# An attention and two-layer-pair kernel: PSUM sums in banks chosen by block, y1 split straight from PSUM, and attention, q and the later layers at other steps of a block

## The chip, the cores and the metric

One core of one Trainium2 chip. The time is device microseconds (us) of one execution, lower is better. Six engines matter: TensorE (PE, with its weight loads PEld), VectorE (DVE), ScalarE (ACT), GpSimd (POOL), and SyncE (SP), whose queue issues the DMAs.

## The reference, cut to what matters

```python
kv_pool = kv.reshape(B, H//r, r, W//r, r, C).mean(axis=(2, 4))   # 768 keys
k = v = kv_pool.reshape(B, -1, C) @ w_sr
a = softmax((q @ k.T) / sqrt(C));  x = a @ v                      # 12288 tokens, C = 128
h = x @ w_in1;  g = max(h, 0) + alpha * min(h, 0);  x = g @ w_out1   # 128 -> 2048 -> 128
h = x @ w_in2;  g = h * sigmoid(1.702 * h);         out = g @ w_out2  # 128 -> 2048 -> 128
```

## The kernel before

The 12288 tokens are worked in 24 blocks of 512. Every product is made of three fp16 matmuls (`mm3`: high by high, high by low, low by high), so each operand is split into a scaled high part (ACT) and a low part (DVE or POOL). A block j has five stages: attention (S, the scores, four sets of 128 tokens; V, the six groups of keys summed into `xacc`), L1 and L2 of the first pair (`h1`, then the sum `y1`), L3 and L4 of the second pair (`h3`, then the sum `y2`). L1 to L4 run over 16 slices m of the 2048 inner columns.

The program is written as steps t, 16 to a block. In step t stands slice m of L1 for t = 16j + m; L2 comes 4 steps later, L3 `L3_LAG` steps later, L4 `L4_LAG` steps later, so that five blocks' stages are mixed: in the middle of the run each step has three matmuls of each of L1, L4, L3 and L2, in this order on PE, 12 of 512 columns, with S or V matmuls between L4 and L3. "Step s" below is s = t mod 16. `ATT_START` is the step at which a block's attention begins, `ATT_S` and `ATT_V` are the places of its S sets and V groups behind that. For each S set DVE takes the maximum (`nm`), ACT the exponential (`s`) with its sum, DVE the reciprocal (`r`), ACT the scaled high part (`ah`), DVE the low part (`al`); both go through transposing DMAs into V's operands.

Before q, `xacc` and `y1` are split, their largest value is taken (`ta` on DVE), spread over the partitions by a one-column matmul (`qt`, `pt`, `yt`), and turned into a power of two. `x_scale` and `x_split`, `a_q` and `q_split`, `y_scale` and `y_split` do this; `parts` makes the two halves (ACT, then DVE).

The eight PSUM banks before: two for S, one (`ps_x`) shared in turn by `xacc`, `qt` and `yt`, two (`ps_y`) shared in turn by `y1` and `y2`, three (`ps_h`) shared in turn by `h1`, `h3` and `pt`. A bank of such a ring is given to the third-next allocation, in the order of the code, once DVE's instruction that reads it last is done (L347 for `h1`, L402 for `h3`). When L2 of a block ends, ACT copies `y1` to SBUF (`yc`, L372) and the split works on the copy.

The framework's scheduler fixes at build time the order of the instructions on each engine; each engine then works strictly in that order and waits for semaphores. POOL makes the low part of `g1` and, for three of four slices, of `g2` (`g1l`, `g2l`); the rest of `g2l` is DVE's.

Of the kernel before, what the change touches and what calls it, by code (L numbers as in the profile page):

```python
# [10 lines left out]
F32 = mybir.dt.float32  # L11
# [23 lines left out]

L2_LAG, L3_LAG, L4_LAG = 4, 31, 36

ATT_START = [-18, -5] + [KF * j - 25 for j in range(2, NB)]  # L40
ATT_S = [(0, 2, 2, 6), (0, 3, 6, 9)] + [(0, 4, 7, 12)] * (NB - 2)
ATT_V = [(5, 8, 9, 12), tuple(range(12, 18))] + [(17, 18, 19, 21, 22, 22)] * (NB - 2)
KV_FREE = -11
W4_LOAD = -8

# [8 lines left out]
def attn_moe_kernel(ctx: ExitStack, tc: tile.TileContext, q, kv, w_sr, w_in1, w_out1, alpha, w_in2, w_out2, out):  # L54
    nc = tc.nc
# [5 lines left out]
    at_p = ctx.enter_context(tc.tile_pool(name="atp", bufs=2))  # L61
    e_p = ctx.enter_context(tc.tile_pool(name="ep", bufs=2))
    t_p = ctx.enter_context(tc.tile_pool(name="tp", bufs=2))
    ps_s = ctx.enter_context(tc.tile_pool(name="ps_s", bufs=1, space=PSUM))
    ps_x = ctx.enter_context(tc.tile_pool(name="ps_x", bufs=1, space=PSUM))
    ps_y = ctx.enter_context(tc.tile_pool(name="ps_y", bufs=2, space=PSUM))

    first = ExitStack()
    ps_w = first.enter_context(tc.tile_pool(name="ps_w", bufs=1, space=PSUM))
    ps_s2 = first.enter_context(tc.tile_pool(name="ps_s2", bufs=1, space=PSUM))  # L70
    ps_h = None

# [19 lines left out]
    kyc = const.tile([P, 1], F32, name="kyc")  # L92
# [9 lines left out]
    def mm3(o, wh, wl, xh, xl, start, stop):  # L102
        mm(out=o, lhsT=wh, rhs=xh, start=start, stop=False)  # L103
        mm(out=o, lhsT=wh, rhs=xl, start=False, stop=False)  # L104
        mm(out=o, lhsT=wl, rhs=xh, start=False, stop=stop)  # L105

    def ts(out, in0, s1, op0, s2=None, op1=None):
        if op1 is None:
            nc.vector.tensor_scalar(out=out, in0=in0, scalar1=s1, scalar2=None, op0=op0)
        else:  # L110
            nc.vector.tensor_scalar(out=out, in0=in0, scalar1=s1, scalar2=s2, op0=op0, op1=op1)

    def small(name, dt=F32, w=1):
        return sm_p.tile([P, w], dt, tag=name, name=name)
# [88 lines left out]
    late = []  # L203
# [5 lines left out]
    qh, ql, qsc, xacc, eh, el, xh, xl, xsc = ({} for _ in range(9))  # L209
# [6 lines left out]
    def q_split(j):  # L216
        src = q_t.pop(j)
        qh[j] = at_p.tile([P, TB], F16, tag="qh", name="qh")
        ql[j] = at_p.tile([P, TB], F16, tag="ql", name="ql")
        c, p = scale_of(qsc[j], ps_x.tile([P, TB], F32, tag="x", name="qt"), None, "q")  # L220
        qsc[j] = p
        late.append(lambda: parts(qh[j], ql[j], src, c))

# [60 lines left out]

    def a_v(j, k):
        if k == 0:
            xacc[j] = ps_x.tile([P, TB], F32, tag="x", name="xacc")
        if j == 0:

            ts_ = slice(k * P, (k + 1) * P)  # L290
            for i in range(KT):
                mm3(xacc[j][:, ts_], v_hi[:, i, :], v_lo[:, i, :], eh[j][:, i, ts_], el[j][:, i, ts_],
                    i == 0, i == KT - 1)
        else:
            mm3(xacc[j], v_hi[:, k, :], v_lo[:, k, :], eh[j][:, k, :], el[j][:, k, :], k == 0, k == KT - 1)
        if k == len(ATT_V[j]) - 1:
            d = small("xd", BF16)
            xsc[j] = d
            late.append(lambda: top_of(xacc[j], d))

    def top_of(x, d):

        a = small("ta")
        nc.vector.tensor_reduce(out=a, in_=x, axis=AX.X, op=ALU.max, apply_absolute_value=True)
        ts(d, a, 2.0 ** -60, ALU.max)

    def scale_of(d, pm, kc, name):

        mm(out=pm[:, 0:1], lhsT=ones, rhs=d, start=True, stop=True)
        p, c = (sm_p.tile([P, 1], I32, tag=name + x, name=name + x, bufs=4) for x in "pc")  # L310

        def f():
            ts(p, pm[:, 0:1].bitcast(I32), 0x7F800000, ALU.bitwise_and)
            ts(c, p, -1.0, ALU.mult, float(268 << 23) if kc is None else kc, ALU.add)

        late.append(f)
        return c.bitcast(F32), p.bitcast(F32)

    def parts(hi, lo, x, c):
        nc.scalar.activation(hi, x, AF.Copy, scale=c)  # L320
        nc.vector.scalar_tensor_tensor(out=lo, in0=x, scalar=c, in1=hi, op0=ALU.mult, op1=ALU.subtract)
# [212 lines left out]
    def at(t, lag):  # L534

        j, m = divmod(t - lag, KF)
        return (j, m) if 0 <= j < NB else None

    def step(t):
        pieces = [(j, t - ATT_START[j]) for j in range(NB) if -8 < t - ATT_START[j] < 26]  # L540
        if x := at(t, L2_LAG):
            l2(*x)
        flush()
        if x := at(t, 2):
            l1_split(*x)
        if x := at(t, L3_LAG + 1):
            l3_act(*x)
        if x := at(t, L3_LAG + 2):
            l3_split(*x)
        if x := at(t, 0):  # L550
            l1(*x)
        if x := at(t, L4_LAG):
            l4(*x)
        flush()
        for j, p in pieces:
            for n, p0 in enumerate(ATT_S[j]):
                if p == p0 + 1:
                    a_e(j, n)
                elif p == p0 + 2:
                    a_h(j, n)  # L560
                elif p == p0 + 3:
                    a_l(j, n)
        flush()
        for j, p in pieces:
            for n, p0 in enumerate(ATT_S[j]):
                if p == p0:
                    a_s(j, n)
            for k, p0 in enumerate(ATT_V[j]):
                if p == p0:
# [75 lines left out]
```

## Time and profile before

| what | before |
|---|---|
| time, median of 3 runs | 1294.55 us (1293.88 to 1294.94) |
| the profiled execution | 1294.28 us, its span from first to last instruction 1292.5 us |
| PE busy | 1228.2 us (95%) |
| ACT busy | 1107.2 us (86%) |
| DVE busy | 1036.0 us (80%) |
| POOL busy | 780.6 us (60%) |
| matmuls | 5784 |
| granted TensorE clock, mean | 0.979 |

Busy is the time in which an engine had an instruction in work, without its waits. Matmuls overlap in the records (a 512-column one is shown with 0.38 us and the next begins 0.21 to 0.22 us later), so PE's idle time is seen better from the starts of neighbours than from the busy share. The kernel has a start (loads, the keys, the weights of the first pair), a ramp in which the blocks fill the steps, 20 or so equal blocks, and a tail in which only the second pair is left.

### The profile page before, as it was taken

To read this page: it belongs to the slowest core of one execution; us is meant where nothing else is said; L and a number is where in the kernel's file an instruction comes from. 1 tells how busy PE (TensorE), PEld (TensorE's weight loads), DVE (VectorE), ACT (ScalarE), POOL (GpSimd) and SP (SyncE) were. 2 spreads that over 40 slices of the span, in tenths; PEclk is the share of its full clock that TensorE was granted. 3 is DMA by queue.
4 is the path that set the end of the run, shared out by engine and by line. 5 is a ranking of instruction groups with operands and counts; after the bars stand their busy time and mean duration, and the time that the engine had idled before them with its cause. 6 is when DMAs were issued, how large, how long until landed. Compare 5 with 4: busy or idle time off the path is not lost.

```text
span 1292.5 us, 18032 instructions
## 1 busy us (share of the span) xinstructions
PE 1228.2 (95%) x5784; PEld 567.1 (44%) x5784; DVE 1036.0 (80%) x1879; ACT 1107.2 (86%) x1964; POOL 780.6 (60%) x670
## 2 busy tenths in 40 slices
PE   3468999999999999999999999999999999999998
PEld 2323444444444444444444444444444444444443
DVE  7988899778788787887887787787888878877666
ACT  1477899899898898898898998998988988988998
POOL 1046535576675676666665665756756666667774
PEclk8678999999999999999999999999999999999999
DMA  9713312122121221211221121221212212110000
GB/s 374 169 43 56 62 33 54 37 41 54 25 54 42 37 54 33 45 42 37 48 48 38 42 54 30 49 47 32 53 33 46 49 32 43 34 37 21 9 9 17
DMA packets 165375, 66.65 MB, mean 52 GB/s; under 512 B 156448, under 2 KB 156576, under 8 KB 164256
## 3 DMA queue, kind: packets, MB, share of 16 engines
q1 hardware_dynamic: 165280, 65.51, 21.9%
q8 instruction: 45, 0.74, 0.2%
q14 instruction: 50, 0.41, 0.1%
HBM read 21.05 MB, written 6.29 MB: 21 GB/s over the span
## 4 chain that ended last, share of the span: by engine, by line
PE 55%; ACT 16%; DVE 13%; issue 5%; DMA 0%; POOLq 0%; ACTq 0%
PE h L103 8%; PE h L105 7%; PE h L104 7%; PE y L104 7%; PE y L105 7%; PE y L103 7%; DVE g L347 4%; ACT g L346 4%; ACT g L401 3%; ACT s L255 3%; DVE g L402 2%; ACT g1h L354 2%; PE xacc L103 2%; PE xacc L104 2%; PE xacc L105 2%
## 5 line engine op out<-in xcount | busy, mean ns | idle before, releaser
L355 POOL TENSOR_TENSOR g1l<-g,g1h 128x512 f16<-128x512 f32 x384 | 457.0, 1196 | 324.9 <-ACT g1h L354 308.8
L411 POOL TENSOR_TENSOR g2l<-g,g2h 128x512 f16<-128x512 f32 x272 | 315.4, 1160 | 120.5 <-ACT g2h L409 110.9
L401 ACT ACTIVATE g<-h,yu 128x512 f32<-128x512 f32 x384 | 269.4, 702 | 103.9 <-PE h L105 100.8
L402 DVE SCALAR_TENSOR_TENSOR g<-g,h 128x512 f32<-128x512 f32 x384 | 262.5, 684 | 110.6 <-ACT g L401 104.9
L347 DVE SCALAR_TENSOR_TENSOR g<-g,oma,h 128x512 f32<-128x512 f32 x384 | 284.9, 742 | 53.1 <-ACT g L346 47.1
L354 ACT CAST g1h<-g 128x512 f16<-128x512 f32 x384 | 244.3, 637 | 7.2 <-PE y L105 5.6
L346 ACT ACTIVATE g<-h 128x512 f32<-128x512 f32 x384 | 236.2, 615 | 15.3 <-PE h L105 8.0
L409 ACT CAST g2h<-g 128x512 f16<-128x512 f32 x384 | 243.8, 635 | 3.3 <-PE y L105 1.2
L104 PE MATMUL y<-g1l,w2h 128*128 128x512 f16 x384 | 145.5, 379 | 8.7 <-POOL g1l L355 8.7
L103 PE MATMUL h<-xh,w1h 128*128 128x512 f16 x384 | 146.5, 383 | 5.2 <-ACT xh L320 4.1
L103 PE MATMUL h<-yh,w3h 128*128 128x512 f16 x384 | 145.2, 378 | 4.2 <-DVE g L347 1.1
L104 PE MATMUL h<-xl,w1h 128*128 128x512 f16 x384 | 146.6, 382 | 1.4
L105 PE MATMUL h<-xh,w1l 128*128 128x512 f16 x384 | 146.7, 382 | 0.0
L103 PE MATMUL y<-g1h,w2h 128*128 128x512 f16 x384 | 145.6, 379 | 1.2 <-ACT g1h L354 1.2
L104 PE MATMUL y<-g2l,w4h 128*128 128x512 f16 x384 | 145.5, 379 | 0.5 <-POOL g2l L411 0.5
L105 PE MATMUL y<-g2h,w4l 128*128 128x512 f16 x384 | 145.5, 379 | 0.0
L105 PE MATMUL y<-g1h,w2l 128*128 128x512 f16 x384 | 145.5, 379 | 0.0
L103 PE MATMUL y<-g2h,w4h 128*128 128x512 f16 x384 | 145.5, 379 | 0.0
L105 PE MATMUL h<-yh,w3l 128*128 128x512 f16 x384 | 145.4, 379 | 0.0
L104 PE MATMUL h<-yl,w3h 128*128 128x512 f16 x384 | 145.3, 378 | 0.0
L245 DVE TENSOR_REDUCE nm<-s 128x1 f32<-128x768 f32 x96 | 91.5, 953 | 14.2 <-PE s L240 10.6
L411 DVE TENSOR_TENSOR g2l<-g,g2h 128x512 f16<-128x512 f32 x112 | 90.0, 804 | 9.7 <-ACT g2h L409 9.7
(227 smaller groups left out, 1664.8 us busy)
## 6 DMA issues: line engine op xcount, KB each, us to landing
q<-in_q SPq DMA_DIRECT2D x24, 256.0 KB, 2.6
kv<-in_kv SPq DMA_DIRECT2D x12, 512.0 KB, 9.9
out<-ob SPq DMA_DIRECT2D x24, 256.0 KB, 2.0
raw_w<-in_moe_w_in SPq DMA_DIRECT2D x4, 1024.0 KB, 9.7
raw_w<-in_moe_w_out SPq DMA_DIRECT2D x4, 1024.0 KB, 6.9
eh<-ah SPq DMA_TRANSPOSE x96, 2.7
wsr<-in_w_sr SPq DMA_DIRECT2D x1, 64.0 KB, 2.7
al<-in_moe_alpha SPq DMA_DIRECT2D x1, 8.0 KB, 1.8
```

The source lines that it names most:

```text
L103: mm(out=o, lhsT=wh, rhs=xh, start=start, stop=False)
L104: mm(out=o, lhsT=wh, rhs=xl, start=False, stop=False)
L105: mm(out=o, lhsT=wl, rhs=xh, start=False, stop=stop)
L245: nc.vector.tensor_reduce(out=nm, in_=s[:, :, 0:HALF], axis=AX.XY, op=ALU.max, negate=True)
L346: nc.scalar.activation(g, h, AF.Relu, scale=-1.0)
L347: nc.vector.scalar_tensor_tensor(out=g, in0=g, scalar=oma[:, m:m + 1], in1=h, op0=ALU.mult, op1=ALU.add)
L354: nc.scalar.copy(hi, g)
L355: nc.gpsimd.tensor_tensor(out=lo, in0=g, in1=hi, op=ALU.subtract)
L401: nc.scalar.activation(g, h, AF.Tanh, scale=ysc[j][:, 0:1])
L402: nc.vector.scalar_tensor_tensor(out=g, in0=g, scalar=1.0, in1=h, op0=ALU.add, op1=ALU.mult)
L409: nc.scalar.copy(hi, g)
L411: e.tensor_tensor(out=lo, in0=g, in1=hi, op=ALU.subtract)
```

## The change

Three things are done.

1. Banks. `ps_x` and `ps_y` become one pool of three banks: `xacc` and `y1` of block j are summed in bank j mod 2 (first the one, then the other), `y2` of every block in the third. `qt` and `yt` go to the ring of three that `h1`, `h3` and `pt` use (before the first step, to the single bank of the start).
2. `y1` is no longer copied to SBUF: `ta` and the split read it from PSUM, the split one step earlier.
3. Steps. L3 and L4 run 28 and 33 steps behind L1, not 31 and 36; the last S set 10 and not 12 steps behind the attention's begin, V one step earlier; q is prepared 8 steps earlier, `x` scaled and split one step earlier.

```diff
-L2_LAG, L3_LAG, L4_LAG = 4, 31, 36
+L2_LAG, L3_LAG, L4_LAG = 4, 28, 33
-ATT_S = [(0, 2, 2, 6), (0, 3, 6, 9)] + [(0, 4, 7, 12)] * (NB - 2)
-ATT_V = [(5, 8, 9, 12), tuple(range(12, 18))] + [(17, 18, 19, 21, 22, 22)] * (NB - 2)
+ATT_S = [(0, 2, 2, 6), (0, 3, 6, 9)] + [(0, 4, 7, 10)] * (NB - 2)
+ATT_Q = [None, (-6, -4), (-6, -4)] + [(-14, -12)] * (NB - 3)
+ATT_V = [(5, 8, 9, 12), tuple(range(12, 18))] + [(16, 17, 18, 19, 20, 21)] * (NB - 2)
...
-    ps_x = ctx.enter_context(tc.tile_pool(name="ps_x", bufs=1, space=PSUM))
-    ps_y = ctx.enter_context(tc.tile_pool(name="ps_y", bufs=2, space=PSUM))
+    ps_a = ctx.enter_context(tc.tile_pool(name="ps_a", bufs=1, space=PSUM))
+    def sums(n, name):
+        return ps_a.tile([P, TB], F32, tag=f"a{n}", name=name)
...
-        c, p = scale_of(qsc[j], ps_x.tile([P, TB], F32, tag="x", name="qt"), None, "q")
+        c, p = scale_of(qsc[j], bank("qt"), None, "q")
...
-            xacc[j] = ps_x.tile([P, TB], F32, tag="x", name="xacc")
+            xacc[j] = sums(j % 2, "xacc")
...
-            y1[j] = ps_y.tile([P, TB], F32, tag="y", name="y1")
+            y1[j] = sums(j % 2, "y1")
...
-            y = y1.pop(j)
-            yc[j] = at_p.tile([P, TB], F32, tag="yc", name="yc", bufs=1)
...
-                nc.scalar.copy(yc[j], y)
-                top_of(y, d)
-            late.append(f)
+            late.append(lambda: top_of(y1[j], d))
-        c, p = scale_of(ysc[j], ps_x.tile([P, TB], F32, tag="x", name="yt"), kyc, "y")
+        c, p = scale_of(ysc[j], bank("yt"), kyc, "y")
...
-        y = yc.pop(j)
+        y = y1.pop(j)
...
-            y2[j] = ps_y.tile([P, TB], F32, tag="y", name="y2")
+            y2[j] = sums(2, "y2")
...
-        for f, lag in ((x_scale, -2), (x_split, -1), (y_scale, L2_LAG + KF), (y_split, L2_LAG + KF + 2)):
+        for f, lag in ((x_scale, -3), (x_split, -2), (y_scale, L2_LAG + KF), (y_split, L2_LAG + KF + 1)):
```

What stands where, at three places. Line numbers of the changed kernel differ: its L351 and L352 are L346 and L347 of before (`h1` read by ACT and DVE), L398 and L399 are L401 and L402 (`h3`), L359 and L406 are the casts L354 and L409, L408 is L411, L423 is L426. The numbers in names tell buffers apart.

First place: DVE from the maximum of `y1` on, in the middle of the run. Before:

```order
L304 TENSOR_REDUCE ta<-y_3358 128x1
L109 TENSOR_SCALAR yd<-ta 128x1
L347 SCALAR_TENSOR_TENSOR g_3955<-g_3955,oma,h_3925 128x512
L245 TENSOR_REDUCE nm<-s 128x1
L109 TENSOR_SCALAR qp<-qt 128x1
L109 TENSOR_SCALAR nm<-nm,qu 128x1
L111 TENSOR_SCALAR qc<-qp 128x1
L111 TENSOR_SCALAR qu<-qp,kq 128x1
L402 SCALAR_TENSOR_TENSOR g_3974<-g_3974,h_3951 128x512
```

and in the changed kernel:

```order
L250 TENSOR_REDUCE nm<-s 128x1
L399 SCALAR_TENSOR_TENSOR g_3941<-g_3941,h_3925 128x512
L114 TENSOR_SCALAR nm<-nm,qu 128x1
L352 SCALAR_TENSOR_TENSOR g_3964<-g_3964,oma,h_3948 128x512
L266 TENSOR_SCALAR r<-sm 128x1
L267 RECIPROCAL r<-r 128x1
L309 TENSOR_REDUCE ta<-y_3396 128x1
L309 TENSOR_REDUCE ta<-q_3686 128x1
L114 TENSOR_SCALAR yd<-ta 128x1
L399 SCALAR_TENSOR_TENSOR g_3978<-g_3978,h_3960 128x512
L285 SCALAR_TENSOR_TENSOR al__4024<-s,r,ah 128x768
L352 SCALAR_TENSOR_TENSOR g_3999<-g_3999,oma,h_3985 128x512
```

The S set whose `nm` came behind the maximum of `y1` now comes ahead of it, its `al` behind it, q's one-column work is gone from here, and the maximum of q has come in. In the changed kernel `yt` takes the bank that the last row here frees.

Second place: ACT where the output `ob` and the copy stand. Before:

```order
L401 ACTIVATE g_3918<-h_3898,yu 128x512
L372 COPY yc<-y_3358 128x512
L354 CAST g1h<-g_3902 128x512
L346 ACTIVATE g_3955<-h_3925 128x512
L409 CAST g2h<-g_3884 128x512
L426 ACTIVATE ob<-y_3377,yu 128x512
L401 ACTIVATE g_3974<-h_3951,yu 128x512
L255 ACTIVATE s,sm<-s,nm,qu 128x2x384
L320 ACTIVATE qh<-q_3341,qc 128x512
```

and in the changed kernel (a later block):

```order
L398 ACTIVATE g_5683<-h_5669,yu 128x512
L274 ACTIVATE ah<-s,r 128x768
L351 ACTIVATE g_5707<-h_5690 128x512
L406 CAST g2h<-g_5650 128x512
L423 ACTIVATE ob<-y_5122,yu 128x512
L359 CAST g1h<-g_5673 128x512
L398 ACTIVATE g_5717<-h_5703,yu 128x512
```

The copy is gone, and `ob`, `qh` and the exponential of the last S set no longer stand together. `ob` empties the one bank that the next block's `y2` begins in one step later.

Third place: DVE around the maximum of `xacc`. Before:

```order
L304 TENSOR_REDUCE ta<-xacc 128x1
L304 TENSOR_REDUCE ta<-q_3949 128x1
L109 TENSOR_SCALAR xd<-ta 128x1
L402 SCALAR_TENSOR_TENSOR g_4342<-g_4342,h_4325 128x512
L109 TENSOR_SCALAR qd<-ta 128x1
L347 SCALAR_TENSOR_TENSOR g_4375<-g_4375,oma,h_4349 128x512
L245 TENSOR_REDUCE nm<-s 128x1
L109 TENSOR_SCALAR xp<-pt 128x1
```

and in the changed kernel:

```order
L326 SCALAR_TENSOR_TENSOR ql<-q_3686,qc,qh 128x512
L309 TENSOR_REDUCE ta<-xacc 128x1
L352 SCALAR_TENSOR_TENSOR g_4343<-g_4343,oma,h_4323 128x512
L114 TENSOR_SCALAR xd<-ta 128x1
L399 SCALAR_TENSOR_TENSOR g_4356<-g_4356,h_4339 128x512
L285 SCALAR_TENSOR_TENSOR al__4407<-s,r,ah 128x768
L352 SCALAR_TENSOR_TENSOR g_4381<-g_4381,oma,h_4363 128x512
L408 TENSOR_TENSOR g2l<-g_4316,g2h 128x512
L114 TENSOR_SCALAR xp<-pt 128x1
```

q's split has moved in ahead of the maximum, and `pt` now falls into a step that has neither S nor V matmuls; because `pt` is in the ring, that step's `h3` takes the bank that the row with `h_4339` frees.

## Rows read from the trace of the kernel before

**Rows 1.** Busy time of each engine in four stretches, granted clock, DMA share and GB/s

```profile
0.00:68.60 68.60, 28.36 (x138) 19.22 (x139) 56.02 (x117) 20.39 (x26) 9.25 (x10) 0.72 0.77 256
68.60:120.00 51.40, 40.37 (x152) 16.52 (x152) 46.35 (x89) 37.94 (x61) 29.30 (x19) 0.84 0.25 49
120.00:154.50 34.50, 31.15 (x148) 14.06 (x148) 27.46 (x56) 27.51 (x51) 19.64 (x17) 1.00 0.32 66
601.00:651.00 50.00, 49.78 (x238) 22.90 (x237) 40.33 (x73) 44.90 (x82) 32.39 (x28) 1.00 0.23 43
```

**Rows 2.** Timeline of PE in one middle block: start, duration, then the instruction

```profile
603.56 0.38 PE L103 MATMUL y<-g2h,w4h 128*128 128x512 f16 x1
604.01 0.38 PE L104 MATMUL h<-xl,w1h 128*128 128x512 f16 x1
...
607.25 0.38 PE L105 MATMUL y<-g2h,w4l 128*128 128x512 f16 x1
607.46 0.38 PE L103 MATMUL y<-g1h,w2h 128*128 128x512 f16 x1
607.86 0.38 PE L103 MATMUL h<-yh,w3h 128*128 128x512 f16 x1
...
618.81 0.38 PE L105 MATMUL y<-g2h,w4l 128*128 128x512 f16 x1
619.10 0.38 PE L103 MATMUL h<-yh,w3h 128*128 128x512 f16 x1
...
621.49 0.38 PE L105 MATMUL y<-g2h,w4l 128*128 128x512 f16 x1
622.00 0.38 PE L103 MATMUL h<-yh,w3h 128*128 128x512 f16 x1
```

**Rows 3.** Timeline of DVE in the same block

```profile
612.47 0.68 DVE L304 TENSOR_REDUCE ta<-y 128x1 f32<-128x512 f32 x1
613.36 0.75 DVE L347 SCALAR_TENSOR_TENSOR g<-g,oma,h 128x512 f32<-128x512 f32 x1
614.03 0.95 DVE L245 TENSOR_REDUCE nm<-s 128x1 f32<-128x768 f32 x1
614.90 0.14 DVE L109 TENSOR_SCALAR qp<-qt 128x1 int32<-128x1 int32 x1
...
619.69 0.68 DVE L402 SCALAR_TENSOR_TENSOR g<-g,h 128x512 f32<-128x512 f32 x1
620.29 1.00 DVE L280 SCALAR_TENSOR_TENSOR al__7101<-s,r,ah 128x768 f16<-128x768 f32 x1
621.21 0.73 DVE L347 SCALAR_TENSOR_TENSOR g<-g,oma,h 128x512 f32<-128x512 f32 x1
```

**Rows 4.** Timeline of ACT in the same block

```profile
615.32 0.96 ACT L255 ACTIVATE s<-s,nm,qu 128x768 f32<-128x768 f32 x1
616.29 0.72 ACT L320 ACTIVATE qh<-q,qc 128x512 f16<-128x512 f32 x1
616.90 0.61 ACT L409 CAST g2h<-g 128x512 f16<-128x512 f32 x1
617.40 0.60 ACT L346 ACTIVATE g<-h 128x512 f32<-128x512 f32 x1
...
618.98 0.91 ACT L269 ACTIVATE ah<-s,r 128x768 f16<-128x768 f32 x1
619.77 0.64 ACT L409 CAST g2h<-g 128x512 f16<-128x512 f32 x1
```

**Rows 5.** Groups by line: count | busy us, mean ns | idle before

```profile
L321 DVE SCALAR_TENSOR_TENSOR yl<-yc,yh 128x512 f16<-128x512 f32 x24 | 26.4, 1099 | 5.2 <-ACT yh L320 5.1
L321 DVE SCALAR_TENSOR_TENSOR xl<-xacc,xc,xh 128x512 f16<-128x512 f32 x24 | 17.9, 744 | 0.9 <-ACT xh L320 0.8
L372 ACT COPY yc<-y 128x512 f32<-128x512 f32 x24 | 14.2, 592 | 0.0
```

**Rows 6.** Waits: who for whom, us in total, times, longest

```profile
PE h L103 <- ACT xh L320: 4.1, 2, 3.0
```

More of the change, by code (lines that the diff above doesn't have):

```diff
@@ L330, in x_split @@
         late.append(lambda: parts(xh[j], xl[j], xa, xsc[j][0]))
-    g1, g2, y1, y2, yh, yl, yc, ysc = ({} for _ in range(8))
+    g1, g2, y1, y2, yh, yl, ysc = ({} for _ in range(7))
     h1, h3, gg = {}, {}, {}
@@ L364, in l2 @@
         if m == KF - 1:
-            y = y1.pop(j)
-            yc[j] = at_p.tile([P, TB], F32, tag="yc", name="yc", bufs=1)
             d = small("yd", BF16)
             ysc[j] = d
-            def f():
-                nc.scalar.copy(yc[j], y)
-                top_of(y, d)
-            late.append(f)
+            late.append(lambda: top_of(y1[j], d))
     def y_scale(j):
-        c, p = scale_of(ysc[j], ps_x.tile([P, TB], F32, tag="x", name="yt"), kyc, "y")
+        c, p = scale_of(ysc[j], bank("yt"), kyc, "y")
         u = sm_p.tile([P, 2], F32, tag="yu", name="yu", bufs=4)
@@ L447, in attn_moe_kernel @@
     kp2 = ps_s2.tile([P, 2, 512], F32, tag="s", name="kp2")
-    pks = [kp2[:, 0, 0:TK], kp2[:, 1, 0:TK], ps_y.tile([P, TB], F32, tag="y", name="pk")[:, 0:TK]]
+    pks = [kp2[:, 0, 0:TK], kp2[:, 1, 0:TK], sums(2, "pk")[:, 0:TK]]
     def thirds(i):
@@ L539, in step @@
     def step(t):
-        pieces = [(j, t - ATT_START[j]) for j in range(NB) if -8 < t - ATT_START[j] < 26]
+        pieces = [(j, t - ATT_START[j]) for j in range(NB) if -16 < t - ATT_START[j] < 26]
         if x := at(t, L2_LAG):
@@ L570, in step @@
                     a_v(j, k)
-            if p == -6 and j > 0:
+            if j > 0 and p == ATT_Q[j][0]:
                 a_q(j)
-            if p == -4 and j > 0:
+            if j > 0 and p == ATT_Q[j][1]:
                 q_split(j)
```

## The prediction

> **What bounds the kernel now.** I first cut the run into stages and read the busy time of each engine [rows 1]; the values stand in the order PE, PEld, DVE, ACT, POOL, then granted clock, DMA share and GB/s. In the start (0 to 68.6 us) DVE has 56.0 us of work and PE 28.4; in the next stretch (68.6 to 120.0, the first block's sixteen steps) DVE 46.4 of 51.4 and PE 40.4; between 120.0 and 154.5 PE has 31.2, DVE 27.5 and ACT 27.5 of 34.5. From then on PE is all but full: in the 50 us of a middle block it is busy 49.8, DVE 40.3, ACT 44.9. So DVE sets the pace of the first 120 us, PE that of all the rest, and a saving on ACT, DVE or POOL in the middle is worth only the PE pauses that it ends.
>
> Then I looked for those pauses in PE's timeline [rows 2]. A matmul is shown with 0.38 us, but the next starts 0.21 to 0.22 later, so a pause is the distance of two starts less 0.215 or so. A middle block, some 50.1 us long, has four:
> - 603.56 to 604.01, at step 0: L1's second matmul waits for `xl`, 0.23;
> - 607.46 to 607.86, at step 1: L3's first waits for a bank of the ring, 0.19;
> - 618.81 to 619.10, at step 5: 0.08;
> - 621.49 to 622.00, at step 6: 0.30, again L3's first at a bank that DVE's L347 frees late.
> Together 0.80 us. Behind the last two lies a jam on DVE and ACT [rows 3, 4]: the maximum of `y1` (0.68) and an S set's maximum `nm` (614.03 to 614.90, 0.87) come close together on DVE, then the exponential (0.97) and `qh` (0.61) on ACT. The reads of `h1` and `h3` queue behind them.
>
> **The change part by part.** The profiled execution took 1294.28 us (span 1292.5 and 1.8 around it), within 0.3 us of the median of 1294.55, so the sum starts at 1294.3.
>
> *What the steady block loses.* `xl` is split a step earlier, which ends the 0.23. q's work and the set of S that met the maximum of `y1` go elsewhere, which should end the other three. All four: −0.80 a block. The least is −0.23, if the jams only move.
>
> *What it gains in waits.* `yt` and `pt` now have little time. I laid the order of the changed kernel out by hand with durations from rows 3 and 4, counting from the first L1 matmul of a step. A step without S or V is 12 matmuls of 0.215, 2.6 us; an S set adds six of 384 columns, an estimated 0.16 each (0.215 × 384/512), 1.0 us.
>
> (a) `yt`. The last S set now stands three steps ahead of `yt`, whose matmul PE reaches at 3.6 + 2.6 + 2.6 + 1.3 (six matmuls of L1 and L4) = 10.0 us. On DVE the S set's `nm` begins at 3.7 (scores done 2.7; the `g1` row, 0.67, and the low part of `g2`, about 0.6, are ahead of it) and leaves at 5.3 with the `g2` row (0.60) behind; the exponential ends at 6.5; `r` and its reciprocal, the maxima of `y1` and q, `yd`, a `g2` row, `al` and a `g1` row (each 0.60 to 0.92 but the small ones) bring it to 10.3. `yd` itself is done earlier, but the bank that `yt` takes is freed by the last rows of this piece: `yt` waits 0.27, and L3's bank behind it another 0.14. About 0.4, between 0.1 and 0.8.
>
> (b) `pt`. It falls into a step with neither S nor V. ACT's tanh is done at 7.7, the exponential (0.97) and `qh` (0.61) by 9.4; then `ql`, the maximum of `xacc`, a `g1` row, `xd` and a `g2` row take DVE to 12.2, where L3 wants its bank at 12.0. About 0.27 with the step after it, between 0 and 0.6.
>
> (c) `ob`. `y2` has one bank now, so the next block's first L4 waits for `ob`. The last L4 of the block is done at 21.3; on ACT `ah` (0.79), a read of `h1` (0.50) and a cast (0.50) come first, then `ob` (an estimated 0.7): 23.07 against 23.01 wanted. About 0.1, between 0 and 0.5.
>
> The sum of (a) to (c) is +0.77, between 0.1 and 1.9. Against −0.80 that leaves −0.03 a block, −0.7 us over some 21 blocks. The banks of `xacc` and `y1` cost nothing by this layout: `y1` is read to the end by its split at about 14.7 after the step of (a) began, and `xacc` of the block after next needs that bank at about 17.8, more than a step later. V a step earlier is covered too: the transposes that feed it have some 4 us in hand.
>
> *ACT's copy and `yl`.* The copy removes 24 × 0.592 = 14.2 us of ACT [rows 5], which is busy 44.9 of 50.0 us and not the bound: nothing, unless a read of `h` queues behind it (that is in the four pauses). `yl` will take what `xl` takes from PSUM, 744 ns against 1099: 24 × 0.355 = 8.5 us of DVE, covered by its 9.7 idle us a block. If `yl` stays at 1099 the only loss is 0.36 behind `yt`, one of the bounds of (a). The Trainium skill ("VectorE: DVE Perf Modes", section "Why PSUM operands drop a tier") says that an operand in PSUM holds a DVE instruction at the slowest rate for fp32, by which reading `y1` from PSUM could win nothing; rows 5 show the read from PSUM 0.36 us shorter, so the measurement decides. By either the term is zero.
>
> *The ramp.* While DVE is the bound, order is worth more. `xh` of two blocks makes PE wait 4.1 us, 3.0 of it once [rows 6]; `x` split a step earlier should end the shorter one, 1.1, and a wait for `xl` of 0.2 beside it: −1.3 (0 to −2; the long one belongs to the start, where DVE decides). L3 and L4 three steps earlier put work into 120.0 to 154.5, where PE has 3.4 us without work and DVE 7.0: −1 (0 to −2). `qt` of the second block no longer waits until the first `xacc` is split, so its first two S sets come earlier into DVE's busiest stretch, or out of the way: −1.5 (−4 to +2). In the start `ql` (about 0.67) comes in, an exponential no longer stands behind an `nm` (0.87): −0.5 (±1.5). Sum −4.3, between −9 and +2.
>
> *The tail* has PE full and keeps the distance of five steps from L3 to L4: zero.
>
> 1294.3 − 0.7 − 4.3 = 1289.3; I say 1289.
>
> **The rivals.** A measurement can tell about 0.2% of this kernel, 2.6 us, from no change: faster is below 1292, slower above 1297.
>
> *The waits vanish.* If (a) to (c) come to 0.3, DVE's rows being early by less than half a us each, the block loses 0.5: 21 × 0.5 = 10.5, and 1294.3 − 10.5 − 4.3 = 1279.5, 1273 to 1284. For it: each of the three is late by 0.1 to 0.3 only, less than one DVE row. Against it: each is on a chain of ten instructions, and PE has no pause to catch up in.
>
> *No change.* The new waits are 0.95 and not 0.77 (+0.15 × 21 = +3 against the net of zero), or the ramp gives nothing because DVE has the same work there: 1292 to 1297. For it: DVE's 46.4 of 51.4 us do not shrink by the change in that stretch but for one row.
>
> *Slower: the third entry of the ring.* Before, a block took 33 places of the ring; now 35. If a DVE row ahead of `yt` is slowed as `yl` is against `xl` (0.36), at the places (a) and (b) alike, each block gains 0.36 to 0.72: +7.5 to +15, and with the ramp's −4.3 the time is 1297 to 1305. It becomes slower when the three waits exceed 0.80 + 4.3/21 + 2.6/21 = 1.13 a block. For it: `yl`'s 1099 ns is beside POOL at work, and DVE's low part of `g2` stands in both places while POOL is busy 32 of 50 us. Against it: that low part is DVE's in one slice of four.
>
> *Slower: the bank of `y1`.* If the split of `y1` slipped by a step and a quarter, more than 3 us, V of the block after next would wait for it, and each further us would cost a us a block. The Trainium skill ("PSUM — Partial Sum Buffer", "Summary: rules for kernel authors") asks to empty PSUM promptly, which the copy did and the change does not. No row shows a slip of that size; the longest pause here is 0.30.
>
> **How the numbers follow.** Forecast, 1284 to 1292: 0.46. Waits vanish, 1273 to 1284: 0.17. No change, 1292 to 1297: 0.21. Slower, by the ring 0.13 and by the bank 0.03: 0.16. Faster is 0.46 + 0.17 = 0.63, same 0.21, slower 0.16. The range leaves out the lower half of the second case (0.08) and most of the fourth (0.12): 1276 to 1298. The likeliest case alone has 1284 to 1292.
>
> **What would show it.** Right, if PE's pauses at step 0 and at the step of `y1`'s maximum are gone, new ones of 0.1 to 0.5 stand at L3's first matmul behind `yt` and `pt` and at L4's first behind `ob`, the block's period stays within 0.1 of 50.1 us, the steps from 120 us on begin some 3 to 5 us earlier, the copy is gone and `yl` is near 744 ns. Wrong, if the period changes by more than 0.2, if V waits for a bank of `y1`, or if the gain comes in the middle and not in the first 155 us. The most doubtful terms are (a), because it is the difference of two sums of ten durations, and the ramp, because there a later row of DVE moves all behind it.

## The result, and the profile after

The change makes the kernel slower: 1308.62 us (median of four runs, 1307.17 to 1309.43) against 1294.74 us of before in the same comparison, a ratio of 1.0104 with an interval of 1.0092 to 1.0117. The profiled execution has a span of 1307.7 us, 15.2 more than before. The prediction said 1289 and faster.

The stages come first, as in [rows 1] (the windows follow the steps, so the first three end where steps 0, 16 and 32 begin; the values stand in the same order).

```profile
0.00:72.60 72.60, 29.87 (x151) 20.04 (x152) 58.75 (x123) 21.96 (x29) 9.19 (x10) 0.76 0.73 245
72.60:119.80 47.20, 32.82 (x139) 13.61 (x138) 45.64 (x86) 35.67 (x56) 27.19 (x17) 0.93 0.26 53
119.80:158.30 38.50, 35.32 (x163) 15.55 (x162) 31.86 (x63) 31.43 (x57) 21.05 (x18) 0.96 0.29 59
600.00:650.00 50.00, 49.37 (x235) 22.59 (x234) 38.95 (x73) 44.19 (x80) 32.08 (x28) 1.00 0.20 42
```

In the middle PE starts 235 matmuls in 50 us where it started 238; DVE and ACT have a little less to do than before and wait more. The period, the distance from one block's first L1 matmul to the next block's, is 50.77 us and was 50.09. The third stage is longer mostly because it holds more (163 matmuls against 148): L3 begins three steps earlier.

Summed over the run from the starts of neighbours, as in [rows 2], PE's lost time before step 0 grows by 2.0 us, in blocks 0 to 2 it is the same to 0.1, in blocks 3 to 21 it grows by 12.9, in the last two by 0.3: 15.2 together. So the loss is 19 blocks of 0.68. (The 2.0 at the start are not more than what the first weights come later: DVE can take them at 9.90 us in this execution and at 7.35 in that of before; in 14 of the 18 experiments they came between 7.2 and 7.9.)

PE's timeline of one block of the changed kernel shows where its pauses are now (start, duration, instruction, and in brackets the idle time before it and who ended it):

```profile
615.22 0.38 PE L110 MATMUL y<-g2h,w4l 128*128 128x512 f16 x1
616.00 0.38 PE L108 MATMUL h<-yh,w3h 128*128 128x512 f16 x1 [0.40 <-DVE g L352]
...
617.72 0.38 PE L110 MATMUL h<-xh,w1l 128*128 128x512 f16 x1
618.17 0.38 PE L108 MATMUL y<-g2h,w4h 128*128 128x512 f16 x1
...
627.34 0.38 PE L110 MATMUL y<-g2h,w4l 128*128 128x512 f16 x1
627.75 0.16 PE L314 MATMUL yt<-yd,ones 128*128 128x1 bf16 x1
...
628.21 0.38 PE L110 MATMUL y<-g1h,w2l 128*128 128x512 f16 x1
628.66 0.38 PE L108 MATMUL h<-yh,w3h 128*128 128x512 f16 x1
...
657.19 0.17 PE L314 MATMUL pt<-xd,ones 128*128 128x1 bf16 x1
657.41 0.38 PE L108 MATMUL h<-yh,w3h 128*128 128x512 f16 x1
```

All four pauses of before are gone. In their place: 0.56 at step 0 (L3 at a bank that L352, DVE's reader of `h1`, frees late), 0.23 at step 1 (L4's first, behind `ob`), 0.19 and 0.23 at step 4 (`yt`, and L3 behind it), 0.20 at step 13 (L3 behind `pt`) and 0.05 at step 14. Together 1.46 us, where the pauses of before, counted in the same way, make 0.77; the difference is that of the periods, to 0.01. The view of waits, over the whole run, has the change of L3's waits in one row; the like row of before, with L347 for L352, had 2.1 us and 5 times.

```profile
PE h L108 <- DVE g L352: 15.6, 25, 2.7
```

The longest pause was not in the forecast. To find its cause, follow DVE and then ACT from step 13 on (rows that the text doesn't use left out):

```profile
608.28 1.67 DVE L408 TENSOR_TENSOR g2l<-g,g2h 128x512 f16<-128x512 f32 x1
609.88 0.14 DVE L114 TENSOR_SCALAR xp<-pt 128x1 int32<-128x1 int32 x1
609.95 0.67 DVE L399 SCALAR_TENSOR_TENSOR g<-g,h 128x512 f32<-128x512 f32 x1
...
611.32 0.94 DVE L250 TENSOR_REDUCE nm<-s 128x1 f32<-128x768 f32 x1
612.19 0.73 DVE L326 SCALAR_TENSOR_TENSOR xl<-xacc,xc,xh 128x512 f16<-128x512 f32 x1
612.85 0.20 DVE L114 TENSOR_SCALAR nm<-nm,qu 128x1 f32<-128x1 f32 x1
...
615.20 0.75 DVE L352 SCALAR_TENSOR_TENSOR g<-g,oma,h 128x512 f32<-128x512 f32 x1 [0.66 <-ACT g L351]
```

```profile
613.08 0.96 ACT L260 ACTIVATE s<-s,nm,qu 128x768 f32<-128x768 f32 x1 [0.53 <-DVE nm L114]
613.97 0.19 ACT L260 ACTIVATION_READ_ACCUMULATOR s<-s,nm,qu 128x1 f32 x1
614.06 0.60 ACT L406 CAST g2h<-g 128x512 f16<-128x512 f32 x1
614.57 0.59 ACT L351 ACTIVATE g<-h 128x512 f32<-128x512 f32 x1
```

The matmuls of the S set end at about 610.4, but DVE comes to its maximum at 611.32, because a low part of `g2` took 1.67 us ahead of it; `xl`, now split here, stands between the maximum and the short row that ends `nm`. The exponential starts at 613.08, and behind it in ACT's order stand a cast and the read of `h1` (614.57), for which L352 and then L3 wait. What delays the low part is seen on POOL:

```profile
605.53 1.16 POOL L360 TENSOR_TENSOR g1l<-g,g1h 128x512 f16<-128x512 f32 x1
608.25 2.73 POOL L360 TENSOR_TENSOR g1l<-g,g1h 128x512 f16<-128x512 f32 x2 [1.56 <-ACT g1h L359]
```

POOL's `g1l` starts 0.03 us before DVE's `g2l`, and the two stand in each other's way. The Trainium skill ("SBUF — State Buffer", section "Who interferes with whom") says that VectorE and GpSimd share a pair of SBUF ports and that only one of them holds it at a time. The rows agree: DVE's instruction ends 0.54 us after the first of POOL's two could have (609.95 against 608.25 + 1.16), and the two take 2.73 us where a single one takes 1.16. Between 150 and 1200 us DVE makes 95 such low parts before and 94 after; before, 72 take about 0.7 and 21 take 1.2, 19 of them at step 12 of a block; after, 73 take about 0.7 and 18 take 1.67, all at step 13.

The three durations are one relation. In the kernel before, the 1.2 and the long `yl` look like this:

```profile
642.48 1.16 POOL L355 TENSOR_TENSOR g1l<-g,g1h 128x512 f16<-128x512 f32 x1 [2.56 <-ACT g1h L354]
642.95 1.23 DVE L411 TENSOR_TENSOR g2l<-g,g2h 128x512 f16<-128x512 f32 x1 [0.28 <-ACT g2h L409]
...
623.07 1.16 POOL L411 TENSOR_TENSOR g2l<-g,g2h 128x512 f16<-128x512 f32 x1 [0.31 <-ACT g2h L409]
623.64 1.13 DVE L321 SCALAR_TENSOR_TENSOR yl<-yc,yh 128x512 f16<-128x512 f32 x1 [0.27 <-ACT yh L320]
```

Both DVE rows end 0.54 us after POOL's instruction does. Over all twenty traces, between 150 and 1200 us, 401 of DVE's low parts start while an instruction of POOL has at least 0.15 us to go, and 396 of them end 0.54 to 0.56 us after it. In the other order nothing is lengthened: the low part that starts 0.07 us ahead of POOL's instruction in the changed kernel takes 0.67 us. So what a meeting costs DVE is what POOL's instruction has left, less some 0.14 us: from nothing to 1.0.

The groups of lines answer to [rows 5]: `yl` from PSUM is as quick as `xl`, and the copy is gone. (In the changed kernel 18 of 21 `yl` start while POOL is at work, and take 0.74 to 0.75 us.)

```profile
L326 DVE SCALAR_TENSOR_TENSOR yl<-y,yc,yh 128x512 f16<-128x512 f32 x24 | 17.8, 743 | 0.0
L326 DVE SCALAR_TENSOR_TENSOR xl<-xacc,xc,xh 128x512 f16<-128x512 f32 x24 | 17.7, 736 | 0.0
L408 DVE TENSOR_TENSOR g2l<-g,g2h 128x512 f16<-128x512 f32 x112 | 96.6, 863 | 1.1 <-ACT g2h L406 1.1
```

### The profile page after: what moved, and what is told of

The parts are those of the page before. It is cut to its first block, busy times and chain, and to the rows that moved or that the text cites. A ratio compares the mean times of both kernels' runs of the same rounds, so it can differ in the third digit from the quotient of the medians.

```text
span 1307.7 us, 17885 instructions
## 1 busy us (share of the span) xinstructions
PE 1228.9 (94%) x5784; PEld 566.9 (43%) x5784; DVE 1023.2 (78%) x1879; ACT 1100.6 (84%) x1940; POOL 787.6 (60%) x670
## 5 line engine op out<-in xcount | busy, mean ns | idle before, releaser
L360 POOL TENSOR_TENSOR g1l<-g,g1h 128x512 f16<-128x512 f32 x384 | 461.8, 1208 | 273.4 <-ACT g1h L359 249.9
L408 POOL TENSOR_TENSOR g2l<-g,g2h 128x512 f16<-128x512 f32 x272 | 315.8, 1162 | 174.4 <-ACT g2h L406 165.9
L398 ACT ACTIVATE g<-h,yu 128x512 f32<-128x512 f32 x384 | 267.1, 696 | 99.7 <-PE h L110 93.7
L399 DVE SCALAR_TENSOR_TENSOR g<-g,h 128x512 f32<-128x512 f32 x384 | 262.3, 683 | 103.3 <-ACT g L398 100.4
L352 DVE SCALAR_TENSOR_TENSOR g<-g,oma,h 128x512 f32<-128x512 f32 x384 | 284.8, 742 | 59.2 <-ACT g L351 56.3
L359 ACT CAST g1h<-g 128x512 f16<-128x512 f32 x384 | 241.5, 630 | 7.9 <-DVE g L352 6.1
L351 ACT ACTIVATE g<-h 128x512 f32<-128x512 f32 x384 | 232.2, 605 | 14.4 <-POOL g1l L360 4.4
L406 ACT CAST g2h<-g 128x512 f16<-128x512 f32 x384 | 240.3, 626 | 3.9 <-PE y L110 1.7
L408 DVE TENSOR_TENSOR g2l<-g,g2h 128x512 f16<-128x512 f32 x112 | 96.6, 863 | 1.1 <-ACT g2h L406 1.1
```

Source lines behind the costliest of these rows:

```text
L351: nc.scalar.activation(g, h, AF.Relu, scale=-1.0)
L352: nc.vector.scalar_tensor_tensor(out=g, in0=g, scalar=oma[:, m:m + 1], in1=h, op0=ALU.mult, op1=ALU.add)
L359: nc.scalar.copy(hi, g)
L360: nc.gpsimd.tensor_tensor(out=lo, in0=g, in1=hi, op=ALU.subtract)
L398: nc.scalar.activation(g, h, AF.Tanh, scale=ysc[j][:, 0:1])
L399: nc.vector.scalar_tensor_tensor(out=g, in0=g, scalar=1.0, in1=h, op0=ALU.add, op1=ALU.mult)
```

## The experiments

Each row of this table is a kernel of its own. The period and the pauses (in us, more than 0.05 each) are those of block 11 of its profile; the ratio is to the kernel before, run beside it.

| kernel | median us | ratio, interval | period | pauses |
|---|---|---|---|---|
| before | 1294.7 | | 50.09 | 0.23, 0.18, 0.07, 0.29 |
| changed | 1308.6 | 1.010 (1.009 to 1.012) | 50.77 | 0.56, 0.23, 0.19, 0.23, 0.20, 0.05 |
| e_x | 1307.8 | 1.009 (1.007 to 1.011) | 50.75 | 0.07, 0.44, 0.35, 0.60 |
| e_g2l | 1300.9 | 1.003 (1.002 to 1.005) | 50.41 | 0.17, 0.09, 0.31, 0.27, 0.28 |
| e_qt | 1309.6 | 1.010 (1.009 to 1.012) | 50.76 | as changed |
| e_banks | 1295.4 | 1.0005 (0.999 to 1.002) | 50.09 | as before |
| b_lag | 1297.2 | 1.0016 (1.001 to 1.003) | 50.21 | 0.18, 0.24, 0.50 |
| b_lagg | 1294.8 | 1.000 (0.999 to 1.001) | 50.15 | 0.24, 0.24, 0.07, 0.29 |
| b_q | 1286.3 | 0.993 (0.992 to 0.995) | 49.71 | 0.24, 0.18 |
| e_lag | 1316.6 | 1.016 (1.015 to 1.018) | 51.17 | 0.10, 1.01, 0.50, 0.28 |
| bq_s | 1291.5 | 0.998 (0.997 to 0.999) | 49.94 | 0.24, 0.09, 0.32 |
| bq_x | 1287.6 | 0.995 (0.993 to 0.996) | 49.77 | 0.30, 0.17 |
| b0_q | 1292.3 | 0.998 (0.997 to 0.999) | 49.92 | 0.24, 0.39 |
| bq_lagg | 1287.1 | 0.994 (0.993 to 0.996) | 49.77 | 0.24, 0.24 |
| e_pool | 1297.2 | 1.002 (1.001 to 1.003) | 50.19 | 0.26, 0.37, 0.20, 0.05 |
| e_lagp | 1302.2 | 1.005 (1.004 to 1.007) | 50.40 | 0.26, 0.10, 0.50, 0.20, 0.06 |
| bq_svx | 1313.8 | 1.015 (1.014 to 1.017) | 51.18 | as e_lag |
| bq_pool | 1283.6 | 0.992 (0.990 to 0.993) | 49.54 | 0.24 |
| bqx_pool | 1284.2 | 0.991 (0.989 to 0.993) | 49.62 | 0.19, 0.14 |
| b0_pool | 1295.9 | 1.000 (0.999 to 1.001) | 50.14 | 0.24, 0.61 |

**e_x**, x's old steps in the changed kernel:

```diff
-for f, lag in ((x_scale, -3), (x_split, -2), ...
+for f, lag in ((x_scale, -2), (x_split, -1), ...
```

> The changed kernel with x scaled and split at the old steps (-2, -1). Theory J (a jam): the 0.56 us pause of L3 at step 0 comes because xc, xh and xl now stand behind the S set of step 14, between its maximum and its exponential, so that ACT reads h1 late; here that pause goes, the 0.23 for xl at step 0 returns, the block shrinks by about 0.33 and the time is 1301 to 1304. Theory R (the ring): qt, pt and yt as extra entries of the ring of three make L3 wait for a younger h1, whatever stands on DVE; then 0.5 of the pause stays and the time is 1308 to 1313.

Both missed. The 0.56 is gone, but the period is the same: the low part of `g2` takes its 1.67 us at step 14 now, L3 waits 0.60 there, and `xl` is waited for 0.44. The jam moved with the order of DVE's rows: x's earlier split decides where the pause falls, not that there is one.

**e_g2l**, another slice for DVE:

```diff
-e = nc.vector if j == 0 or m % 4 == 3 or ...
+e = nc.vector if j == 0 or m % 4 == 2 or ...
```

> The changed kernel, but DVE makes the low part of g2 for slices m % 4 == 2 instead of 3, so at steps 0, 4, 8, 12 (as before the change) and not 1, 5, 9, 13. Theory J: the low part at step 13 (1.67 us beside POOL) is the other half of the jam; without it the maximum of the S set comes 0.5 to 0.8 earlier, the pause at step 0 falls to under 0.2, but the wait at yt (step 4) may grow by 0.2: block -0.2 to -0.5, time 1299 to 1305. Theory R: no change at step 0, 1306 to 1310.

As theory J said in time, and the pause at step 0 is gone. On DVE only an idle time and one `g` row stand right ahead of the S set's maximum:

```profile
604.49 0.21 DVE L116 TENSOR_SCALAR xc<-xp,kxc 128x1 int32<-128x1 int32 x1
605.50 0.75 DVE L352 SCALAR_TENSOR_TENSOR g<-g,oma,h 128x512 f32<-128x512 f32 x1 [0.81 <-ACT g L351]
606.17 0.95 DVE L250 TENSOR_REDUCE nm<-s 128x1 f32<-128x768 f32 x1
```

But a low part at step 5 takes 1.37 us now, and L3 and L1 wait 0.31 and 0.27 at steps 5 and 6.

**e_qt**, `qt` of the first two blocks in the empty second sum bank:

```diff
-c, p = scale_of(qsc[j], bank("qt"), None, "q")
+c, p = scale_of(qsc[j], sums(1, "qt") if j < 2 else bank("qt"), None, "q")
```

> The changed kernel, but qt of the first two blocks goes into the second sum bank, which is empty then, and not into the one bank of the start, where it waits for pm. If that wait is what made the start longer (step 0 at 72.6 instead of 68.6 us), step 0 comes at 68.5 to 70 and the time is 1304 to 1306. If the start is longer because the first weights land later (DVE's first maximum of w1 at 9.9 instead of 7.35 us), it stays at 71 to 73 and the time at 1307 to 1309. The pauses of the middle blocks stay as they are by either.

Neither reading held in full. Step 0 came at 69.8, but what was won there was gone by step 32 (158.2 against 158.3 us), and the time did not move: the start is not where the loss is, and the earlier step 0 was worth nothing here. (The first weights came 2.7 us earlier than in the changed kernel's profile, at 7.18 us, so this run doesn't show what `qt`'s place alone did for step 0.)

**e_banks**, the new banks with all steps as before:

```diff
-L2_LAG, L3_LAG, L4_LAG = 4, 28, 33
+L2_LAG, L3_LAG, L4_LAG = 4, 31, 36
-ATT_S ... (0, 4, 7, 10)
+ATT_S ... (0, 4, 7, 12)
-ATT_Q ... [(-14, -12)]     -ATT_V ... [(16, 17, 18, 19, 20, 21)]
+ATT_Q ... [(-6, -4)]       +ATT_V ... [(17, 18, 19, 21, 22, 22)]
-... (x_scale, -3), (x_split, -2), ... (y_split, L2_LAG + KF + 1)
+... (x_scale, -2), (x_split, -1), ... (y_split, L2_LAG + KF + 2)
```

> The banks alone: new banks, qt, pt and yt in the ring, y1 split from PSUM and no copy, but all steps (lags, S, V, q, x, y) as before the change. Theory J: the steps carry the loss; the old four pauses (0.80) stay, ob on its single bank adds 0.1 to 0.2 and yt's bank up to 0.2: 1297 to 1302. Theory R: the banks carry it, with the same +0.7 a block as the whole change: 1306 to 1312.

Better than theory J: period and pauses are those of before to 0.01 us. `qt` and `yt` in the ring, `y2` on one bank and `y1` split from PSUM cost nothing at the old steps. Theory R, by which the ring alone makes the loss, is out: it comes with the steps. Whether the new steps would lose as much on the old banks was not tried; the waits at `yt` and `pt` are for banks of the ring.

**b_lag** and **b_lagg**, the lags alone on e_banks, without and with DVE's slice moved:

```diff
-L2_LAG, L3_LAG, L4_LAG = 4, 31, 36
+L2_LAG, L3_LAG, L4_LAG = 4, 28, 33
 (b_lagg only)
-m % 4 == 3
+m % 4 == 2
```

> The banks alone (period 50.09 us, as before the change) plus the lags 28 and 33, nothing else. Theory G: the lags carry the loss, since three steps less move DVE's own low part of g2 from steps 0, 4, 8, 12 to 1, 5, 9, 13, ahead of the maxima of S at steps 7, 11, 14 and of y1: the period rises by 0.4 to 0.8 and the time is 1303 to 1311. Rival A: the attention's steps, q and x carry it; the lags alone leave the period within 0.1 to 0.2 (ob's bank), 1294 to 1299.

> The kernel b_lag with DVE's slice of g2 put back to steps 0, 4, 8, 12 (m % 4 == 2). Theory G: the period comes back to within 0.2 of 50.09, 1293 to 1298. If the lags cost by something else (y2's bank, another order of L3 among the rows of DVE), it stays where b_lag is.

Rival A was right: the lags cost 0.12 a block, with the slice moved 0.06. No low part is longer than 0.69 us in b_lag's block.

**b_q**, q alone on e_banks:

```diff
-[(-6, -4)] * (NB - 3)
+[(-14, -12)] * (NB - 3)
```

> The banks alone plus q prepared eight steps earlier, nothing else. q's one-column work and qh leave the place where y1's maximum, an S set and qh meet (pauses of 0.07, 0.02 and 0.29 at steps 5 and 6). If qh and qt were what made that jam, these 0.38 go: period 49.7 to 49.8, time 1286 to 1289. If y1's maximum and the S set alone make it, or q's work jams elsewhere, the period stays within 0.15 of 50.09, 1292 to 1298.

The first reading held, 0.38 a block: the jam at steps 5 and 6 needed q's work. This one part of the change is worth 0.7%.

**e_lag**, the changed kernel with the old lags:

```diff
-L2_LAG, L3_LAG, L4_LAG = 4, 28, 33
+L2_LAG, L3_LAG, L4_LAG = 4, 31, 36
```

> The changed kernel with the old lags 31 and 36: the new banks, and the new steps of S, V, q, x and y. Theory G: with the low part of g2 back at steps 0, 4, 8, 12 the block is at most what the changed kernel with the moved slice showed (1.17 us of pauses), less ob's 0.17: period 50.1 to 50.3, time 1294 to 1300. Rival A: the steps carry the loss, period 50.6 to 50.8, 1305 to 1310.

Theory G fell, and rival A was too low: the old lags make it worse, and DVE's low part meets POOL again, at step 1 (first DVE, then ACT, then PE):

```profile
615.75 1.67 DVE L408 TENSOR_TENSOR g2l<-g,g2h 128x512 f16<-128x512 f32 x1
...
618.61 0.94 DVE L250 TENSOR_REDUCE nm<-s 128x1 f32<-128x768 f32 x1
```

```profile
619.83 0.96 ACT L260 ACTIVATE s<-s,nm,qu 128x768 f32<-128x768 f32 x1 [1.08 <-DVE nm L114]
...
622.90 0.91 ACT L274 ACTIVATE ah<-s,r 128x768 f16<-128x768 f32 x1
...
624.67 0.72 ACT L423 ACTIVATE ob<-y,yu 128x512 f32<-128x512 f32 x1
```

```profile
625.44 0.38 PE L108 MATMUL y<-g2h,w4h 128*128 128x512 f16 x1 [0.85 <-ACT ob L423]
```

The S set's matmuls end at 617.4, its maximum starts 1.2 later, ACT idles 1.08 for it and then has no gap left until `ob`, for which PE waits.

**bq_s** and **bq_x**, single parts on b_q:

```diff
 (bq_s)
-(0, 4, 7, 12)
+(0, 4, 7, 10)
 (bq_x)
-(17, 18, 19, 21, 22, 22)   -(x_scale, -2), (x_split, -1)
+(17, 18, 19, 20, 21, 21)   +(x_scale, -3), (x_split, -2)
```

> The banks and q's earlier steps (period 49.71, 1286 us) plus the last S set at 10 instead of 12, nothing else. Theory S: this set carries the loss: its exponential and its ah and al now fall on steps 2 to 4, where ob, y1's maximum and yt stand; L4 waits for ob and L3 for the bank behind yt, 0.7 to 1.4 a block: 1301 to 1315. Rival X: x and V a step earlier carry it; then this kernel stays within 0.2 a block of its base, 1283 to 1291.

> The banks and q's earlier steps plus x scaled and split one step earlier, for which V's six groups are drawn together to 17, 18, 19, 20, 21, 21; the S sets stay. By theory S the pause of 0.24 for xl goes and pt adds at most 0.28 at step 13, as in the changed kernel with the old lags: -0.24 to +0.1 a block, 1281 to 1289. By rival X the period rises by 0.4 or more, 1294 to 1310.

S alone costs 0.23, a third or less of what theory S said, and just over rival X's bound; x, with V drawn together, costs 0.06 and so is no rival. Together with V's and y's steps they cost 1.46 (e_lag against b_q): the parts that were timed do not add up. V at its new step alone was not.

**b0_q**, q's earlier steps in the kernel before (old banks):

```diff
...
-if p == -6 and j > 0:
+if j > 0 and p == (-14 if j > 2 else -6):
     a_q(j)
-if p == -4 and j > 0:
+if j > 0 and p == (-12 if j > 2 else -4):
     q_split(j)
```

> The kernel before, old banks, with nothing but q prepared eight steps earlier. qt then shares its bank with the xacc that is being summed. If the gain of the earlier q needs the new banks, PE waits for that bank each block, 0.4 us or far more: 1300 or above. If only the places on DVE and ACT matter and qt can stand until the bank is free, 1285 to 1290 as with the new banks.

Between the two: 0.2% of the 0.7%. The 0.24 at step 0, now at `qt`, stands in b_q too, for `xl`; what differs is L3's pause behind it, 0.39 against 0.18. So q's move wants the new banks for the larger part of its gain.

**bq_lagg**, b_q with the new lags and DVE's slice moved:

```diff
-L2_LAG, L3_LAG, L4_LAG = 4, 31, 36
+L2_LAG, L3_LAG, L4_LAG = 4, 28, 33
-m % 4 == 3
+m % 4 == 2
```

> The banks, q's earlier steps, lags 28 and 33, and DVE's slice m % 4 == 2: the best parts so far together. The lags alone took 0.6 us from the banks alone in the start and the tail and cost 0.05 a block; if that adds up, the period is 49.7 to 49.8 and the time 1284 to 1287. If the lags and q's work meet (qh and qt at steps 3 to 5 beside ob), the period is 49.9 or more, 1290 or above.

The period is as said, the gain of the start isn't there; the lags are worth nothing.

**e_pool**, **e_lagp** and **bq_pool**, DVE's low parts given to POOL in the changed kernel, in e_lag and in b_q:

```diff
-e = nc.vector if j == 0 or m % 4 == 3 or j == NB - 1 and m % 2 else nc.gpsimd
+e = nc.vector if j == 0 or j == NB - 1 and m % 2 else nc.gpsimd
```

> The changed kernel, but POOL makes the low part of g2 for all slices (the first block and half of the last apart), DVE none. Theory C (collision): the 1.67 us that this one DVE instruction takes at step 13, where 0.68 is usual, makes the jam that ends in L3's 0.56 pause at step 0; it goes, and the wait behind yt shrinks since one row less is ahead of nm: period 50.0 to 50.4, time 1292 to 1301. Rival D (the places themselves): x, S and y at their new steps jam with or without it; only 0.61 of DVE is freed where the pause is 0.56 with others behind it, period 50.5 to 50.8, 1303 to 1309. Rival P: POOL, at 69% of the span instead of 60%, becomes late, PE waits for g1l and g2l: 1310 or above.

> The changed kernel with the old lags (period 51.17, 1316.6 us) and all of g2's low parts on POOL. There DVE's low part takes 1.67 us at step 1, just ahead of the maximum of the S set at step 1. Theory C: that delay runs through the exponential and ah to ob, for which L4 waits 1.0; without it the period is 50.0 to 50.4, 1292 to 1300. Rival D: 50.7 or more, 1306 or above.

> The banks and q's earlier steps (period 49.71, 1286 us), the best so far, with all of g2's low parts on POOL. There DVE's low part meets POOL only at step 8 (1.23 us), where PE has no pause. Theory C: nothing or little to win, period 49.5 to 49.75, 1282 to 1288. Rival P: PE waits for POOL, 1290 or above.

Theory C held in e_pool (0.58 of a block's 0.68 gone; the pause at step 0 falls from 0.56 to 0.26, and L4 no longer waits for `ob`). In e_lagp the period ends at 50.40, the upper end of C, and the time two us above it; the wait for `ob` falls from 1.01 to 0.10. In the control there is no collision in a place that matters, and the gain is 0.17. POOL is not late: with 36.8 of 50 us at work it is not waited for in the block, and PE is busy 49.92 (49.78 in [rows 1], 49.91 in b_q).

```profile
550.00:600.00 50.00, 49.92 (x241) 23.18 (x240) 37.28 (x70) 45.13 (x82) 36.76 (x34) 1.00 0.20 43
```

**bq_svx**, e_lag with y's old split:

```diff
-(y_split, L2_LAG + KF + 1)
+(y_split, L2_LAG + KF + 2)
```

> The changed kernel with the old lags and y split at its old step (two steps after yt); the rest of the new steps stays, so that against the banks and the earlier q only S, V and x differ. S alone cost 0.23 a block and x with a drawn-together V 0.06; together with y's split they cost 1.46. If the split of y a step earlier is what is missing, the period is 49.9 to 50.2, 1290 to 1297. By theory C the missing part is the 1.67 us collision at step 1, ahead of y's place, and nearly all of it stays: 50.9 to 51.2, 1309 to 1317.

As theory C said: all of it stays, the 1.67 with it. By the period y's earlier split costs nothing (51.17 and 51.18); the medians are 2.8 us apart, the intervals of the ratios overlap, and the profiled execution here, 1317.2 us, is the longest of its four.

**bqx_pool**, bq_x with the low parts on POOL, and **b0_pool**, the kernel before with them on POOL:

> The best so far (banks, q's earlier steps, all of g2's low parts on POOL; period 49.54, 1283.6 us, one pause of 0.24 for xl left) plus x a step earlier with V drawn together. If only the rows ahead of pt matter, the 0.24 goes and at most the 0.17 at pt takes its place: period 49.3 to 49.5, 1278 to 1283. If L3's wait at step 1 (0.30 without POOL's help) stays, 49.6 to 49.8 and 1284 to 1288.

> The kernel before with only the low parts of g2 all on POOL. Its collision (1.23 us at step 12) is not followed by a pause, so by theory C little comes of it; but DVE loses 0.6 us of work at step 4, ahead of the jam at steps 5 and 6 (0.07, 0.02 and 0.29): period 49.8 to 50.1, 1287 to 1295. If POOL becomes late, 1296 or above.

In bqx_pool the pause for `xl` goes, and 0.19 at `pt` and 0.14 behind it take its place: period and time fall into the second reading, but not by its cause, a wait of L3 at step 1; and the time is no better than bq_pool's. In b0_pool the time freed on DVE, four low parts a block, brings nothing, just less than was expected (the time lies between the two readings): 0.18 at step 1 goes, and 0.07 and 0.29 become one pause of 0.61 at step 5. So time freed on DVE is not by itself what e_pool won.

## Why the prediction was wrong

**What bounds the kernel** was read rightly: PE is full in the middle, and only pauses count. Between the forecast of 1289.3 and the profiled execution of 1309.4 us lie 20.1: 13.6 in blocks 3 to 21 (+12.9 where −0.7 was forecast), 6.3 up to block 2, 0.3 in the tail.

**The banks** were put at zero, and that is what e_banks measured, `y1`'s bank included: no V group waits for it in the middle of the run. Of the two readings of `yl` from PSUM the row was right (743 ns; forecast 744), and as forecast it was worth nothing, and the copy's 14.2 us of ACT too. That PSUM is the quicker source was not what the two rows showed, though: `yl` of before is long because it meets POOL, and the one that doesn't, between 150 and 1200 us, takes 0.74.

**The pauses removed**: all four are gone, as forecast, and b_q shows that q's move alone ends 0.38 of the 0.80.

**(a) and (b)** were right in place and size: 0.43 for about 0.4, and 0.25 for about 0.27. For (a) some of that is luck: without the low part that the working has ahead of `nm` it is still 0.37 (e_pool). **(c)**, `ob`, was 0.23 for 0.1, within its bounds; it is zero in e_pool, but 0.17 in e_g2l, where no low part is long ahead of it, so the 1.67 alone doesn't explain the surplus.

**The step that failed** is the sum of the new waits, "+0.77, between 0.1 and 1.9". It has three places, and the dearest pause is at a fourth: 0.56 at step 0. I counted x's earlier split as a pause removed (−0.23) and did not lay out the rows that it joins, the S set of step 14 and, through the lag, the low part of `g2` at step 13. The price of such a row was taken as 0.6 us; beside POOL it is 1.67 here. The new waits came to 1.46 and not 0.77, and a block to +0.68 and not −0.03. I had named that slowing as a rival, at the places of `yt` and `pt` and with 0.36 a row, from `yl` against `xl`. That was one instance of a delay that runs from nothing to 1.0 us with the moment of the meeting, and it came at another place. The rival's time (1297 to 1305) lay nearest to the result, but the two more entries of the ring that it was hung on cost nothing by themselves (e_banks).

What the loss is made of follows by differences: q's earlier steps −0.38 a block (b_q against e_banks), the other new steps +1.06 (the changed kernel against b_q). Without DVE's low parts the same step from b_q to the changed kernel is +0.65 (bq_pool to e_pool). The remaining 0.41 goes with DVE's low part. Two runs speak for the collision and against the freed time: b0_pool, where the low parts leave without a gain, and e_g2l, where DVE keeps all four of a block at other steps and 0.36 is gained. The 0.65 are the waits of (a) and (b) and 0.26 at step 0, with the low part gone, less the 0.24 for `xl`; what makes the 0.26 was not tested. Why S, V and x cost 1.46 together and 0.29 singly is shown only so far that the 1.67 stands in e_lag and bq_svx and not in bq_s or bq_x, and that 0.77 of it goes with DVE's low parts (51.17 to 50.40); how the rest falls on the pairs was not separated.

**The ramp** was forecast at −4.3, and is the second term that failed: lost time up to block 2 is 2.0 us more than before in the profiled execution, the upper bound that was given (the bounds of its four terms add up to −10 and +3, not −9 and +2). Step 32 begins 3.8 us later (with three more slices of L3 ahead of it), where 3 to 5 earlier was forecast. Late weights are in that; e_g2l, e_x and e_pool, whose weights came in time and whose start is all but that of the changed kernel, have 0.5 less, 0.3 more and 0.3 more, e_qt has 1.8 more, e_banks none, b_q 2.8 less. So the terms that I listed are not borne out: with x's steps and lags of before, b_q has the largest gain. What each of them was worth was not separated.

**A version better than both kernels** is bq_pool: the new banks, q eight steps earlier, all other steps as before, and all of `g2`'s low parts on POOL: 1283.6 us, 0.9915 of before (0.990 to 0.993). One pause a block is left, 0.24 for `xl`.

## What to carry to other kernels

Lay out a moved step not only where its own result is waited for, but on every in-order queue that it joins, with the rows that it is now next to: here the forecast of three places was good to some 0.1 us and the fourth, not laid out, decided. A row's duration belongs to its place: the same DVE subtraction took 0.68, 1.23 or 1.67 us by what POOL did at that moment, and moving whole stages by a step moves such meetings about. When several parts come in one change, time each alone: here the banks cost nothing, one part gave 0.7% and the rest took 1.7%.

## What was not expected of the hardware

That a meeting of DVE and POOL costs as much as this, and depends on hundredths of a us: the low part that starts 0.03 us behind POOL's instruction (608.28 and 608.25) takes 1.67 us, one that starts 0.07 ahead of it 0.67. One that meets POOL later in its work takes 1.2, by the same relation. And that reading one operand from PSUM made `yl` shorter, not longer: it fell from 1099 to 743 ns, the duration of `xl`, because it no longer waits for POOL. In the traces of before and after, between 150 and 1200 us, of DVE's rows of 512 or 768 columns only those with both such operands in SBUF (the low parts of `g2`, and `yl` of before) are lengthened when POOL is at work; the rows that read `h`, `s` or `y1` from PSUM are not.
